# A new order for one block's list of steps in a convolution and SiLU MLP kernel

## The chip, the cores and the metric

The kernel runs on one core of a Trainium2 chip. The metric is the device time of one execution in microseconds; before the change it is 2363.76 us, the median of three runs (2363.1 to 2364.65). TensorE (PE) multiplies matrices, VectorE (DVE) and ScalarE (ACT) work elementwise, GpSimd (POOL) issues the accumulating DMAs of the convolution, and SyncE (SP) issues the other DMAs. Each engine works through its own instructions in order, and engines wait for each other by semaphores.

## The reference

```python
def _attn_ref(x, weight):             # x (8, 4096, 192), weight (8 heads, 7 taps)
    w = softmax(weight, axis=-1)
    x_pad = concatenate([zeros((B, 6, D)), x], axis=1)
    x_unf = x_pad[:, idx, :].reshape(B, S, K, H, group)
    return einsum('hk,bskhg->bshg', w, x_unf).reshape(B, S, D)

def _moe_ref(x, w_in, w_out):         # x (32768, 192), w_in (192, 2048), w_out (2048, 192)
    h = x @ w_in
    g = h * (1.0 / (1.0 + exp(-h)))
    return g @ w_out
```

A causal convolution of seven taps, with one set of weights per head, feeds an MLP with SiLU. All is float32.

## The kernel before

The 32768 tokens are worked in 32 blocks of 1024, each as two strips of 512 (the two halves of the partitions). The up product (192 to 2048) and the down product (2048 to 192) are done with schemes that need fewer multiplications than the plain product and more additions.

The program of a block is a list of short tokens, PLAN. A token names a step and, behind the point, its arguments; a sign in front says which block it belongs to: none is the current block, "-" the one before, "=" two before, "+" the next. The list is run once for each value of b from 3 to 33; START is the same kind of list for what comes ahead. A token whose step is done is skipped. `step` (from L856) calls the functions. Every engine's order is the order in which the list mentions its instructions, so a new list is a new order on every engine and on both DMA queues; within one list there are no other costs or due times.

The tokens:

- P*r*.*g* (`product`, L605 to L640): the up product number r of group g. It uses 64 rows of the array, half A or half B; B has r = 0, 1, 2, 4, 5, 6, 11, 14 (but 14 of group 4 is on A). The two halves work at the same time. Each product is two passes of 512 columns. L.*nk* (`plain`): a plain product, either 512 columns on A, or 256 on each half.
- Three chains of products per group add into one PSUM bank each: 5, 2, 6, 1, 0, 14 (first chain), 3, 9, 7, 4, 8 (second), 12, 10 (third). After most links the bank is read before the next link may add to it: u*o*.*g* (L679) copies the first chain's bank to one of ten buffers on ScalarE, X*o*.*g* and a*o*.*g* (L673) add the second chain's bank to such a copy on VectorE, b*o*.*g* subtracts the third's. S*o*.*g* (L691) and SL are the SiLUs on ScalarE. The groups come in the order 0, 4, 1, 2, 3; banks are shared between them, so P5.2 waits for S3.4, and P5.0 of the next block for S3.3.
- t.*ji* (L714): four sums of SiLU results for each of four j on VectorE, two in one tile. These tiles and the output tile share a ring of three buffers.
- D*i*.*je* (`out_slot`, L746): the down products, 128 rows by 32 columns in four column groups, eight passes each (i = 5 is a quarter as long). D4 and D5 need t of their j, D2 needs t.*j*1, D3 needs t.*j*2 and t.*j*3, D0 and D1 need none.
- z, y, x (ScalarE) and M (VectorE, L824): the accumulators of the down products are merged; o (L834) transposes the result, st (L843) stores it from SyncE.
- ld (L181, SyncE): loads of a later block's tokens; i (L465, VectorE): their transposes; ha (L480 to L487): the six tokens ahead of the block, a POOL copy and a small SyncE DMA.
- v.*ki* (`conv`): tap i of channel third k. For i = 0 ScalarE writes the scaled row (L496); for the others it writes one of the ten buffers that the copies u use too (L499), and a POOL DMA adds that buffer to the row (L500). The buffers go round first in, first out.
- sp (L521, SyncE): the convolved rows are spread to the layout of the products; w (L538, L541, VectorE): differences and sums of these.

In short, a block's up half (P, L, u, X, a, b, S) is followed by its down half (D, t, M), and the taps, loads and spreads of later blocks run beside both.

The lines that turn the list into steps are these; the bars in PLAN split it into slots, which are run one after another.

```python
plan = [slot.split() for slot in PLAN.split("|")]
BACK = {"-": 1, "=": 2, "+": -1}
for t in START.split():
    step(2, t)
for b in range(3, NB + 2):
    for s in plan:
        for t in s:
            step(b, t)
```

Of the kernel before, what the change touches and what calls it, by code (L numbers as in the profile page):

```python
# [17 lines left out]
def kernel(  # L18
# [60 lines left out]


    PLAN = (
        "+ld.1 P5.0 | -P8.3 -S1.4 -a0.2 -S4.3 | -D0.00 -t.01 -S0.2 | -D1.00 -S1.2 =o.2 v.00 "
        "| -D2.01 -t.03 -S5.1 =st.2 | -D2.00 -b5.3 | -D1.20 -sp.0 v.21 -S5.3 | -D4.01 u5.0 "
        "-t.02 -S1.3 | -D5.01 -sp.2 | -D4.00 -t.10 | -D0.20 -t.11 | -D3.01 | -D0.11 -t.12 | "
        "-D1.30 v.22 | -D3.00 +ld.2 -t.13 | -D2.11 -a0.3 | -D5.00 | -D2.10 -t.20 -S0.3 | "
        "-D3.11 v.11 | -D5.10 | -D4.11 -w.0 | -D0.30 v.12 | -D4.10 -t.21 | -D1.11 -t.23 | "
        "-D0.21 | -D0.01 v.23 -w.1 | -D3.10 -t.22 | -D5.21 | -D0.31 | -D5.11 | -D1.10 -t.30 "
        "| -D1.01 -t.31 | -D2.20 | -D2.21 v.13 | -D5.20 | -D4.21 v.01 v.14 | -D4.20 v.24 | "
        "-D1.21 -w.2 | -D3.20 -t.33 | -D2.30 v.02 | -D1.31 -t.32 | -D2.31 -y1.0 | -D5.30 "
        "v.03 | -D0.10 v.25 | -D3.21 -z1.0 v.15 -y0.0 | -D4.31 -y2.0 -w.3 | -D5.31 -M1.0 | "  # L90
        "-D3.30 -x2.1 v.26 -x2.0 | -D4.30 -x2.2 -M2.0 | -D3.31 -w.5 -x0.0 -M3.0 | L.02 | "
        "P2.0 -x2.3 -w.4 | P5.4 | P3.0 u4.0 -M6.0 | L.12 v.16 u5.4 | L.00 | P6.0 -x1.0 -M4.0 "
        "| L.10 u2.0 | P2.4 | L.01 X2.0 | L.11 v.04 u4.4 | P9.0 | P1.0 SL.0 -M5.0 SL.2 | "
        "P6.4 | P13.0 u0.0 X4.0 SL.1 | P5.1 | P3.4 -M7.0 S2.0 +i.2 u2.4 | P0.0 | P7.0 X2.4 | "
        "P11.0 | P12.0 u1.0 a5.0 -o.1 | P9.4 | P1.4 S4.0 b1.0 -st.1 u5.1 | P13.4 | P4.0 X4.4 "
        "u0.4 | P10.0 | P2.1 a1.0 +ld.0 v.05 | P7.4 | P0.4 u4.1 b5.0 | P14.0 | P8.0 u1.4 "
        "v.06 S5.0 | P11.4 | P14.4 a5.4 S3.0 a0.0 S2.4 | P6.1 | P12.4 S3.4 | P4.4 | P3.1 "
        "u2.1 b1.4 S4.4 | P5.2 | P10.4 X2.1 | P1.1 a1.4 u5.2 | P9.1 b5.4 | P2.2 u0.1 | P8.4 "
        "X4.1 | P5.3 u4.2 | P7.1 a0.4 | P0.1 +i.1 u5.3 sp.1 | P12.1 a5.1 | P6.2 u1.1 | P3.2 "
        "-o.0 | P4.1 u2.2 b1.1 | P13.1 | P2.3 a1.1 | P10.1 S2.1 | P1.2 u4.3 X2.2 | P8.1 | "  # L100
        "P11.1 -o.3 u0.2 | P13.2 S1.1 a0.1 | P6.3 S4.1 | P9.2 +i.0 | P0.2 b5.1 u2.3 +ha.0 | "
        "P3.3 S0.0 X4.2 | P1.3 S2.2 | P12.2 u1.2 | P11.2 X2.3 | P7.2 u0.3 b1.2 | P14.1 S4.2 "
        "| P9.3 a5.2 S0.4 | P0.3 -st.0 | P10.2 S1.0 X4.3 | P14.2 u1.3 | P7.3 b5.2 +v.20 "
        "-st.3 | P4.2 S0.1 | P12.3 a5.3 S3.1 | P14.3 +v.10 a1.2 | P13.3 | P4.3 S5.2 b1.3 | "
        "P8.2 S2.3 | P11.3 a1.3 S3.3 | P10.3 S5.4 t.00 S3.2"
    )
    START = (
        "=dp.28 =v.20 =v.10 =dp.44 =v.00 =dp.18 =dp.6 =dp.40 =dp.7 =dp.32 =dp.23 =dp.30 "
        "=dp.13 =dp.2 =dp.20 =dp.24 =dp.15 =dp.35 =dp.14 =dp.33 =dp.11 -ld.1 =dp.37 =dp.36 "
        "=dp.25 -ld.2 =dp.27 =dp.17 -ld.0 =dp.0 =v.11 =dp.34 =v.01 =dp.26 =v.12 =dp.29 =v.21 "  # L110
        "=v.13 =dp.45 =v.22 =dp.21 =v.02 =dp.42 =v.14 =v.03 =dp.39 =v.15 =dp.3 =v.04 =dp.38 "
        "=v.16 =dp.47 =v.23 =sp.1 =v.05 =dp.1 =v.24 =dp.22 -i.1 =dp.12 =v.25 =v.06 =dp.43 "
        "=v.26 =go.2 =sp.0 =dp.19 -i.0 =dp.46 -i.2 =dp.31 -ha.0 =dp.9 =sp.2 =dp.4 =dp.41 "
        "-v.10 -v.00 -v.11 =dp.8 -v.20 -v.01 =dp.5 -v.12 =dp.16 -v.02 =w.0 =dp.10 =w.1 =cp.0 "
        "-L.01 -P5.0 -v.03 =cp.1 -L.02 -P5.4 =w.2 -u5.0 -L.10 =w.3 -u5.4 -P2.0 -P3.0 -v.13 "
        "-P2.4 -u4.0 -v.04 -P6.0 -L.00 -u4.4 -L.12 -u2.0 -L.11 -SL.0 -X2.0 -P6.4 -SL.2 =w.4 "
        "=cp.2 -P9.0 -P1.0 -u2.4 =o.0 -P13.0 -P5.1 -v.14 -u0.0 -X4.0 -P3.4 -P1.4 -S2.0 =w.5 "
        "-SL.1 -P7.0 -P11.0 -u5.1 -X2.4 -u0.4 -P12.0 -P0.0 -a5.0 -v.21 -P13.4 -P0.4 -u1.0 "
        "=o.1 -P4.0 -P9.4 -u1.4 -v.15 -S4.0 -P2.1 -P14.4 -a1.0 -b1.0 -P14.0 -P8.0 -u4.1 -X4.4 "
        "-S3.4 -P6.1 -P10.0 -v.22 -S2.4 -a0.0 -P11.4 -P7.4 -u2.1 -b5.0 -S3.0 -P5.2 -P3.1 "  # L120
        "-S4.4 -a5.4 -P1.1 -P12.4 -u5.2 -X2.1 -P4.4 -u0.1 -P9.1 -b1.4 -P2.2 -a1.4 -P10.4 "
        "-X4.1 -P5.3 -u4.2 -P8.4 =o.2 -P6.2 -b5.4 -P13.1 -u5.3 =st.2 -a0.4 -P0.1 -P7.1 -u2.2 "
        "-v.23 -S2.1 ld.1 -P2.3 -P3.2 -a5.1 -u1.1 -S0.0 -P1.2 -P12.1 -X2.2 -S0.4 -P4.1 -u4.3 "
        "-P13.2 -b1.1 ld.2 -S1.4 -P6.3 -a1.1 -u0.2 -P10.1 -v.24 -P11.1 -u2.3 -P8.1 -b5.1 "
        "-P0.2 -S4.1 -P9.2 -v.05 -S2.2 -a0.1 -P12.2 -P1.3 -u1.2 -X4.2 -S0.1 -P3.3 -P14.1 "
        "-b1.2 -u0.3 -S5.4 -P7.2 -P11.2 -X2.3 -v.16 -P10.2 -P0.3 -S4.2 -a5.2 -sp.1 -P9.3 "
        "-P14.2 -u1.3 -b5.2 -S3.1 -P13.3 -P4.2 -X4.3 -S3.2 -S1.0 i.1 -P14.3 -P12.3 =st.0 "
        "-S1.1 -a1.2 -P11.3 -P7.3 -S5.0 -v.06 -S1.2 -t.00 -D0.00 =st.1 -S3.3 -S2.3 -D1.20 "
        "-b1.3 -S5.1 ld.0 -S4.3 -t.01 -D0.01 -S5.2 -D0.21 -t.02 -D1.11 -sp.0 -a5.3 -D1.10 "
        "-v.25 -t.03 -P8.2 P5.0 +ld.1 -P4.3 -P10.3 -D1.30 -b5.3 -v.26 -D1.00 -a0.2 -sp.2 "  # L130
        "-D4.01 -t.10 -S0.2 -D5.00 -D2.01 i.0 -D4.00 -t.11 -D2.00 i.2 -D5.01 ha.0 -t.13 "
        "-D0.11 -D3.00 -a1.3 +ld.2 -D3.01 -t.12 v.10 -D4.11 -w.0 v.00 +ld.0 -D5.10 v.11 v.20 "
        "-D5.11 -D2.10 u5.0 -t.20 -D0.20 -w.1 -D3.11 -t.21 -D4.10 -w.2 -D2.11 -t.23 -P8.3 "
        "P2.0 -D0.31 -a0.3 -t.22 -D3.10 -S0.3 -S1.3 -D4.21 v.21 -S5.3 u4.0 v.01 -D4.20 -t.30 "
        "-D3.20 -D5.21 -t.31 -D2.20 -D5.20 -D2.21 -D0.10 -t.32 -D2.30 v.02 -D1.01 -t.33 "
        "-D0.30 v.03 -D1.31 v.12 -D2.31 v.04 v.22 -D1.21 v.05 -D3.30 -y1.0 -w.3 -z1.0 -D5.30 "
        "v.13 -D5.31 -D3.31 -x2.0 -M1.0 -x2.1 -D4.31 -x2.2 v.14 -x2.3 -y2.0 -M2.0 -D3.21 "
        "-y0.0 v.06 -D4.30 -x0.0 -w.4 v.23 -x1.0 P3.0 P5.4 -M3.0 L.10 u5.4 -w.5 P6.0 L.02 "
        "-M4.0 L.11 u2.0 L.00 P2.4 X2.0 P1.0 L.01 -M5.0 u4.4 v.15 L.12 u0.0 P6.4 P9.0 SL.2 "
        "SL.0 P0.0 P13.0 X4.0 SL.1 u2.4 -M7.0 P3.4 P5.1 S2.0 +i.0 P7.0 P1.4 u5.1 X2.4 P12.0 "  # L140
        "P11.0 u0.4 a5.0 u1.0 v.24 P9.4 P2.1 S4.0 b1.0 P4.0 P13.4 u4.1 X4.4 P14.0 P10.0 a1.0 "
        "P0.4 P7.4 S3.0 b5.0 v.25 P11.4 P8.0 u1.4 a5.4 S2.4 P6.1 P12.4 a0.0 P14.4 P4.4 u2.1 "
        "b1.4 v.26 P5.3 P3.1 S3.4 a1.4 S4.4 P10.4 P1.1 X2.1 P5.2 P8.4 -M6.0 u0.1 b5.4 P9.1 "
        "P0.1 u5.2 -o.1 u5.3 P13.1 P2.2 X4.1 -st.1 u1.1 +i.2 P12.1 P2.3 u4.2 a0.4 S2.1 P7.1 "
        "P6.2 b1.1 u4.3 P3.2 a5.1 P6.3 u2.2 P10.1 S5.4 X2.2 P4.1 u2.3 S0.4 P9.2 b5.1 P1.2 "
        "S0.0 a1.1 P13.2 P11.1 S1.0 -o.0 u0.2 P8.1 v.16 P1.3 S2.2 S4.1 sp.1 P0.2 P12.2 a0.1 "
        "u0.3 X4.2 S5.0 P3.3 P14.1 u1.2 +i.1 P7.2 P11.2 X2.3 -st.0 b1.2 P9.3 P0.3 S4.2 a5.2 "
        "+ha.0 P10.2 u1.3 X4.3 P4.2 S0.1 P7.3 b5.2 P14.3 S1.1 a1.2 S3.1 P12.3 P14.2 S3.3 a5.3 "
        "P13.3 -o.3 P4.3 S3.2 b1.3 -st.3 +v.10 P8.2 +v.20 a1.3 P10.3 P11.3 S5.2 t.00 S2.3"
    )  # L150
    QUEUE = (0, 4, 1, 2, 3)
    CHAIN_BANKS = ((0, 1, 7, 1, 0), (2, 3, 2, 3, 2), (4, 4, 4, 4, 4))
# [41 lines left out]
    x0 = x.flatten_outer_dims()[TB - pad : TB, :].rearrange("t (k c) -> c k t", k=NK)  # L194
# [651 lines left out]
                )  # L846
            )

    plan = [slot.split() for slot in PLAN.split("|")]
    did, later = set(), []  # L850
    closing = f"S3.{QUEUE[-1]}"
    BACK = {"-": 1, "=": 2, "+": -1}
# [263 lines left out]
```

## Time and profile before

| | |
|---|---|
| time, median of three | 2363.76 us |
| span of the profiled execution | 2358.8 us |
| TensorE busy | 2350.1 us (100%), 17630 matmuls |
| VectorE busy | 1784.5 us (76%) |
| ScalarE busy | 1488.6 us (63%) |
| GpSimd busy | 531.0 us (23%) |
| granted TensorE clock | 0.999 of full speed |
| one regular block: up half, down half | 36.26 us, 36.12 us |

The profiled execution's own time is shown by its span alone, from the first to the last instruction; it is 5.0 us below the median of the runs. In a group of instructions the columns are line, engine, operation, tiles, shape and count, then busy time, mean duration in ns, and the idle time before them with what ended it. A line of waits has the total, the number and the longest. A line of the timeline has start and duration in us, engine, line, operation, tiles and, in brackets, the idle time before it and what ended that. PEld is the load of a matmul's weights.

### The profile page before, as it was taken

How to read it: one execution, taken by the hardware profiler on the slowest of the kernel's cores; microseconds unless marked ns; L12 is line 12 of the kernel's file. 1: busy time of each engine (PE TensorE's matmuls, PEld its weight loads, DVE VectorE, ACT ScalarE, POOL GpSimd, SP SyncE). 2: the span in 40 equal slices, each digit the busy share in tenths (PEclk: the TensorE clock that was granted, in tenths of full speed). 3: DMA queues.
4: the chain of work that ended last, by engine and by line, in shares of the span. 5: the costliest groups of instructions: out<-in, count | busy, mean ns of one | idle time of the engine just before them, and what ended most of it. 6: DMA issues, size and time to landing. Idle time of an engine off the chain costs nothing.

```text
span 2358.8 us, 45531 instructions
## 1 busy us (share of the span) xinstructions
PE 2350.1 (100%) x17630; PEld 1053.1 (45%) x17630; DVE 1784.5 (76%) x2373; ACT 1488.6 (63%) x2779; POOL 531.0 (23%) x672
## 2 busy tenths in 40 slices
PE   9999999999999999999999999999999999999998
PEld 4344444444444444444444454444444444444445
DVE  8898767787777787777877777767778777787676
ACT  5346766667656677566676666765667756667643
POOL 4911122211222112222112221122211222211200
PEclk9999999999999999999999999999999999999999
DMA  7234667656566655666556656556655566565511
GB/s 158 51 66 72 107 106 125 105 103 107 98 121 107 106 105 95 119 116 106 106 106 109 119 99 109 105 99 122 107 106 101 101 116 116 106 109 98 96 23 25
DMA packets 523833, 238.81 MB, mean 101 GB/s; under 512 B 431648, under 2 KB 436768, under 8 KB 523616
## 3 DMA queue, kind: packets, MB, share of 16 engines
q0 software_dynamic: 73024, 133.73, 33.7%
q1 hardware_dynamic: 447392, 101.78, 23.1%
q8 instruction: 138, 2.26, 0.4%
q10 hardware_dynamic: 3200, 0.39, 0.1%
q14 instruction: 79, 0.65, 0.1%
HBM read 31.46 MB, written 25.17 MB: 24 GB/s over the span
## 4 chain that ended last, share of the span: by engine, by line
PE 98%; DVE 1%; DMA 0%; ACT 0%; SPq 0%; issue 0%; ACTq 0%
PE ps L746 47%; PE ps L630 42%; PE ps L647 5%; PE ps L767 2%; PE ps L576 2%; PE ps L1015 1%; DVE t L714 0%; DMA dup<-nat 0%; PE ps L423 0%; ACT g L691 0%; DMA nat<-u 0%; SPq L843 0%; DVE g L673 0%; DVE cmb L163 0%; ACT u L163 0%
## 5 line engine op out<-in xcount | busy, mean ns | idle before, releaser
L500 POOL DMA_DIRECT2D nat<-u x504 | 431.9, 957 | 1598.0 <-ACT u L499 643.4
L630 PE MATMUL ps<-win,wr 64*128 64x512 f32 x1550 | 721.5, 598 | 0.0
L746 PE MATMUL ps<-g,wo 128*32 128x512 f32 x2976 | 703.0, 593 | 0.0
L630 PE MATMUL ps<-win,ws 64*128 64x512 f32 x1550 | 638.3, 599 | 0.9 <-ACT u L679 0.9
L746 PE MATMUL ps<-t,wo 128*32 128x512 f32 (+2 forms) x4528 | 547.8, 446 | 0.0
L679 ACT COPY u<-ps 128x512 f32<-128x512 f32 x775 | 442.5, 587 | 136.7 <-PE ps L630 88.6
L746 PE MATMUL ps<-t,wx 128*32 128x512 f32 x2976 | 495.6, 592 | 0.6 <-DVE t L714 0.5
L630 PE MATMUL ps<-dup,wr 64*128 64x512 f32 x868 | 424.1, 597 | 0.0
L691 ACT ACTIVATE g<-g 128x512 f32<-128x512 f32 x465 | 286.2, 633 | 175.5 <-DVE g L673 175.5
L714 DVE TENSOR_TENSOR t<-g,t 128x1024 f32<-128x1024 f32 x248 | 302.0, 1218 | 109.7 <-PE ps L746 107.4
L714 DVE TENSOR_TENSOR t<-g 128x1024 f32<-128x1024 f32 x248 | 302.5, 1220 | 103.9 <-PE ps L746 82.7
L809 ACT COPY yx<-ps 32x512 f32<-32x512 f32 x150 | 86.8, 579 | 421.5 <-PE ps L746 419.4
L673 DVE TENSOR_TENSOR g<-u,ps 128x512 f32<-128x512 f32 x465 | 314.2, 681 | 42.8 <-PE ps L630 32.0
L499 ACT ACTIVATE u<-xt,taps 128x512 f32<-128x512 f32 x504 | 340.0, 717 | 1.1
L630 PEld LDWEIGHTS ps<-win,wr 64*128 64x128 f32 x1550 | 272.1, 186 | 139.5 <-issue 75.6
L630 PE MATMUL ps<-dup,ws 64*128 64x512 f32 x682 | 328.2, 598 | 0.0
L630 PEld LDWEIGHTS ps<-win,ws 64*128 64x128 f32 x1550 | 255.8, 186 | 135.3 <-issue 58.6
L746 PEld LDWEIGHTS ps<-t,wo 128*32 128x32 f32 x4528 | 188.5, 110 | 273.3 <-issue 266.0
L691 ACT ACTIVATE g<-ps 128x512 f32<-128x512 f32 x465 | 267.8, 599 | 36.2 <-PE ps L630 33.6
L673 DVE TENSOR_TENSOR ps<-u,ps 128x512 f32<-128x512 f32 x310 | 215.0, 694 | 64.3 <-PE ps L630 26.7
L746 PE MATMUL ps<-g,wx 128*32 128x512 f32 x1488 | 250.5, 592 | 0.0
L824 DVE TENSOR_TENSOR cmb<-cmb,ps 96x512 f32<-96x512 f32 x150 | 102.2, 681 | 181.7 <-ACT yx L809 180.7
(92 smaller groups left out, 2010.5 us busy)
## 6 DMA issues: line engine op xcount, KB each, us to landing
nat<-u POOLq DMA_DIRECT2D x504, 256.0 KB, 4.0
dup<-nat SPq DMA_DIRECT2D x345, 128.0 KB, 3.0
nat<-in_x_dram SPq DMA_DIRECT2D x382, 64.0 KB, 2.7
out_dram<-osb SPq DMA_DIRECT2D x376, 64.0 KB, 2.0
raw<-in_moe_w_out_dram SPq DMA_DIRECT2D x8, 384.0 KB, 3.5
raw<-in_moe_w_in_dram SPq DMA_DIRECT2D x12, 192.0 KB, 4.4
ws<-wr POOLq DMA_DIRECT2D x8, 192.0 KB, 5.0
raw<-in_moe_w_in_dram SPq DMA_DIRECT2D x6, 128.0 KB, 3.0
```

Of the source, the lines that this page charges most:

```text
L499: pin(nc.scalar.activation(z, src, AF.Copy, scale=tap))
L500: pin(nc.gpsimd.dma_start(out=dst, in_=z, accum_op=ALU.add))
L576: nc.tensor.matmul(hs[a, n, e], rows(wr[j], e)[:, a, k, :], rows(d, e)[:, n, k, :], start=k == 0, stop=k == NK - 1,)
L630: nc.tensor.matmul(to[:, cols], raw(g, *LEFT[e][r], e), rhs[:, cols], start=first, stop=True, skip_group_check=True,)
L647: nc.tensor.matmul(banks[PLAIN_BANKS[n and 1 + e]][:, cols], rows(wr[j] if own == e else ws[j], e)[:, a, k, :], rows(dups[b], e)[:, SLOT[e ...
L673: pin(nc.vector.tensor_tensor(out_, u, v, op=op))
L679: pin(nc.scalar.copy(us[b, g, o][:, cols], t1[:, cols]))
L691: pin(nc.scalar.activation(h, src, AF.Silu))
L714: pin(nc.vector.tensor_tensor(t[i // 2][:, i % 2, :], u, v, op=ALU.subtract))
L746: nc.tensor.matmul(accs[b][at][SQ * q : SQ * q + SQ, to], lhs[:, e, SQ * k : SQ * k + SQ], rhs[:, e, ts(q, TB // 4) if i == 5 else to], st ...
L809: pin(nc.scalar.copy(to, acc[3 * (name[0] == "x") + k][n:P, :]))
L824: pin(nc.vector.tensor_tensor(out_, u, v, op=ALU.add))
```

## The change

PLAN, the list of a block, is replaced by another order of the same 300 tokens, without bars, and START gets five more tokens at its end (the new list has them in another iteration). The list is now split at blanks. START is otherwise the same text in lines of other lengths, cut here to its end. No step is added, removed or altered.

```diff
--- before.py
+++ after.py
@@ -79,74 +79,69 @@


     PLAN = (
-        "+ld.1 P5.0 | -P8.3 -S1.4 -a0.2 -S4.3 | -D0.00 -t.01 -S0.2 | -D1.00 -S1.2 =o.2 v.00 "
-        "| -D2.01 -t.03 -S5.1 =st.2 | -D2.00 -b5.3 | -D1.20 -sp.0 v.21 -S5.3 | -D4.01 u5.0 "
-        "-t.02 -S1.3 | -D5.01 -sp.2 | -D4.00 -t.10 | -D0.20 -t.11 | -D3.01 | -D0.11 -t.12 | "
-        "-D1.30 v.22 | -D3.00 +ld.2 -t.13 | -D2.11 -a0.3 | -D5.00 | -D2.10 -t.20 -S0.3 | "
-        "-D3.11 v.11 | -D5.10 | -D4.11 -w.0 | -D0.30 v.12 | -D4.10 -t.21 | -D1.11 -t.23 | "
-        "-D0.21 | -D0.01 v.23 -w.1 | -D3.10 -t.22 | -D5.21 | -D0.31 | -D5.11 | -D1.10 -t.30 "
-        "| -D1.01 -t.31 | -D2.20 | -D2.21 v.13 | -D5.20 | -D4.21 v.01 v.14 | -D4.20 v.24 | "
-        "-D1.21 -w.2 | -D3.20 -t.33 | -D2.30 v.02 | -D1.31 -t.32 | -D2.31 -y1.0 | -D5.30 "
-        "v.03 | -D0.10 v.25 | -D3.21 -z1.0 v.15 -y0.0 | -D4.31 -y2.0 -w.3 | -D5.31 -M1.0 | "
-        "-D3.30 -x2.1 v.26 -x2.0 | -D4.30 -x2.2 -M2.0 | -D3.31 -w.5 -x0.0 -M3.0 | L.02 | "
-        "P2.0 -x2.3 -w.4 | P5.4 | P3.0 u4.0 -M6.0 | L.12 v.16 u5.4 | L.00 | P6.0 -x1.0 -M4.0 "
-        "| L.10 u2.0 | P2.4 | L.01 X2.0 | L.11 v.04 u4.4 | P9.0 | P1.0 SL.0 -M5.0 SL.2 | "
-        "P6.4 | P13.0 u0.0 X4.0 SL.1 | P5.1 | P3.4 -M7.0 S2.0 +i.2 u2.4 | P0.0 | P7.0 X2.4 | "
-        "P11.0 | P12.0 u1.0 a5.0 -o.1 | P9.4 | P1.4 S4.0 b1.0 -st.1 u5.1 | P13.4 | P4.0 X4.4 "
-        "u0.4 | P10.0 | P2.1 a1.0 +ld.0 v.05 | P7.4 | P0.4 u4.1 b5.0 | P14.0 | P8.0 u1.4 "
-        "v.06 S5.0 | P11.4 | P14.4 a5.4 S3.0 a0.0 S2.4 | P6.1 | P12.4 S3.4 | P4.4 | P3.1 "
-        "u2.1 b1.4 S4.4 | P5.2 | P10.4 X2.1 | P1.1 a1.4 u5.2 | P9.1 b5.4 | P2.2 u0.1 | P8.4 "
-        "X4.1 | P5.3 u4.2 | P7.1 a0.4 | P0.1 +i.1 u5.3 sp.1 | P12.1 a5.1 | P6.2 u1.1 | P3.2 "
-        "-o.0 | P4.1 u2.2 b1.1 | P13.1 | P2.3 a1.1 | P10.1 S2.1 | P1.2 u4.3 X2.2 | P8.1 | "
-        "P11.1 -o.3 u0.2 | P13.2 S1.1 a0.1 | P6.3 S4.1 | P9.2 +i.0 | P0.2 b5.1 u2.3 +ha.0 | "
-        "P3.3 S0.0 X4.2 | P1.3 S2.2 | P12.2 u1.2 | P11.2 X2.3 | P7.2 u0.3 b1.2 | P14.1 S4.2 "
-        "| P9.3 a5.2 S0.4 | P0.3 -st.0 | P10.2 S1.0 X4.3 | P14.2 u1.3 | P7.3 b5.2 +v.20 "
-        "-st.3 | P4.2 S0.1 | P12.3 a5.3 S3.1 | P14.3 +v.10 a1.2 | P13.3 | P4.3 S5.2 b1.3 | "
-        "P8.2 S2.3 | P11.3 a1.3 S3.3 | P10.3 S5.4 t.00 S3.2"
+        "v.01 -S4.3 -P13.3 -P10.3 -sp.2 v.11 P5.0 -a1.3 -P8.3 v.02 -t.00 -t.01 -a0.2 -D1.31 "
+        "-D0.01 =st.1 -S5.1 -D1.11 -S5.4 -D1.00 -D1.20 -S2.3 -D2.01 -D0.21 -t.02 -t.03 -D2.00 "
+        "-S0.2 -D3.01 -b5.3 -t.10 v.22 -t.11 -D2.10 -D5.00 -D0.11 -D1.10 -D4.01 -a0.3 -D3.00 "
+        "-S0.3 v.12 -D4.00 v.13 v.23 -D0.30 v.24 -t.13 -D0.20 -D0.00 -S1.3 -S1.2 v.03 v.04 "
+        "-D5.01 -D4.10 -D4.11 -t.12 -D3.11 -S5.3 -D2.11 -t.20 -t.21 -D0.31 -sp.0 -w.0 -D5.10 "
+        "-D0.10 -y0.0 -D3.10 -D2.21 -D5.11 -D2.20 -t.23 -D4.21 -D1.21 v.14 v.15 -D1.01 -w.1 "
+        "-D4.20 -t.22 -D3.21 -w.2 -t.30 -D1.30 u5.0 -z1.0 -D5.20 -w.3 -w.5 v.05 -t.31 -t.33 "
+        "-D5.31 v.25 v.06 -w.4 -D5.30 -D5.21 -x2.1 +ld.2 -D2.31 +ld.0 +i.0 +ld.1 -y1.0 -D2.30 "
+        "-t.32 -x2.2 -D3.31 -M1.0 -M2.0 -y2.0 -M6.0 v.26 -x2.0 v.16 -D3.30 -D3.20 -D4.30 -D4.31 "
+        "-x1.0 P2.0 L.02 -x2.3 u4.0 P5.4 -M3.0 -M4.0 -x0.0 +i.2 P3.0 L.01 P6.0 u5.4 u2.0 -o.1 "
+        "X2.0 L.00 SL.0 -M5.0 L.12 P2.4 u4.4 L.11 L.10 SL.1 +i.1 -M7.0 SL.2 P1.0 u0.0 P9.0 P6.4 "
+        "u2.4 P13.0 X4.0 S2.0 P5.1 u5.1 P3.4 -o.2 P7.0 P0.0 u1.0 X2.4 P11.0 S4.0 P12.0 a5.0 "
+        "P9.4 P1.4 u0.4 P4.0 P13.4 P2.1 b1.0 P10.0 X4.4 P7.4 a1.0 P0.4 -st.2 -o.3 u4.1 S2.4 "
+        "u1.4 P8.0 b5.0 S5.0 P11.4 P6.1 a5.4 a0.0 P12.4 b1.4 u2.1 P14.4 P14.0 S3.4 P3.1 S3.0 "
+        "P4.4 P5.2 S4.4 X2.1 P10.4 u5.2 P1.1 u0.1 a1.4 P9.1 S1.4 b5.4 -st.3 P8.4 P2.2 u4.2 P0.1 "
+        "X4.1 P7.1 a0.4 S0.4 a5.1 S0.0 u1.1 P12.1 b1.1 P5.3 u5.3 P6.2 u2.2 +ha.0 P13.1 S2.1 "
+        "P4.1 P3.2 S1.0 a1.1 X2.2 P2.3 u4.3 P11.1 +v.00 sp.1 P10.1 P8.1 a0.1 P1.2 -o.0 -st.0 "
+        "b5.1 S4.1 P6.3 P9.2 X4.2 u0.2 P13.2 u2.3 P0.2 S2.2 P3.3 P1.3 P12.2 P7.2 P11.2 X2.3 "
+        "u1.2 P14.2 b1.2 P9.3 u0.3 P0.3 P10.2 +v.20 a5.2 P4.2 S4.2 X4.3 P7.3 S0.1 P14.1 u1.3 "
+        "P14.3 +v.10 b5.2 P12.3 S3.3 S3.2 a1.2 P8.2 +v.21 a5.3 P4.3 S1.1 S3.1 b1.3 P11.3 S5.2"
     )
     START = (
...
-        "P13.3 -o.3 P4.3 S3.2 b1.3 -st.3 +v.10 P8.2 +v.20 a1.3 P10.3 P11.3 S5.2 t.00 S2.3"
...
+        "b5.2 P14.3 S1.1 a1.2 S3.1 P12.3 P14.2 S3.3 a5.3 P13.3 -o.3 P4.3 S3.2 b1.3 -st.3 +v.10 "
+        "P8.2 +v.20 a1.3 P10.3 P11.3 S5.2 t.00 S2.3 -o.2 -st.2 S1.4 +v.00 +v.21"
     )
     QUEUE = (0, 4, 1, 2, 3)
     CHAIN_BANKS = ((0, 1, 7, 1, 0), (2, 3, 2, 3, 2), (4, 4, 4, 4, 4))
@@ -846,7 +841,7 @@
                 )
             )

-    plan = [slot.split() for slot in PLAN.split("|")]
+    plan = [PLAN.split()]
     did, later = set(), []
     closing = f"S3.{QUEUE[-1]}"
     BACK = {"-": 1, "=": 2, "+": -1}
```

## The prediction

> **What bounds the kernel now.** I read the page first, then busy time by stretch, groups by shape, waits, and the timeline of single products.
>
> ```profile
> PE 2350.1 (100%) x17630; PEld 1053.1 (45%) x17630; DVE 1784.5 (76%) x2373; ACT 1488.6 (63%) x2779; POOL 531.0 (23%) x672
> ...
> PE 98%; DVE 1%; DMA 0%; ACT 0%; SPq 0%; issue 0%; ACTq 0%
> ...
> nat<-u POOLq DMA_DIRECT2D x504, 256.0 KB, 4.0
> ...
> out_dram<-osb SPq DMA_DIRECT2D x376, 64.0 KB, 2.0
> ```
>
> TensorE is the chain. But "busy" counts a moment in which one half of the array works and the other waits, so 100% hides what a new order can win. The stretches of one regular block (14), up half and down half, and the end of the one and start of the next:
>
> ```profile
> 1046.56:1082.82 36.26, 36.26 (x172) 20.13 (x168) 30.17 (x47) 30.91 (x59) 4.37 (x6) 1.00 0.52 90
> 1082.82:1118.94 36.12, 36.12 (x385) 12.04 (x384) 23.89 (x26) 16.95 (x31) 11.19 (x13) 1.00 0.68 119
> ```
>
> The first column is the length. A block is 72.38 us at full clock (1.00). In the up half VectorE (30.17) and ScalarE (30.91) are close behind TensorE.
>
> ```profile
> L630 PE MATMUL ps<-win,wr 64*128 64x512 f32 x1550 | 721.5, 598 | 0.0
> L679 ACT COPY u<-ps 128x512 f32<-128x512 f32 x775 | 442.5, 587 | 136.7 <-PE ps L630 88.6 <-DMA nat<-u 28.3 <-ACT yx L804 6.2
> L673 DVE TENSOR_TENSOR g<-u,ps 128x512 f32<-128x512 f32 x465 | 314.2, 681 | 42.8 <-PE ps L630 32.0
> L499 ACT ACTIVATE u<-xt,taps 128x512 f32<-128x512 f32 x504 | 340.0, 717 | 1.1
> ```
>
> ```profile
> PEld ps L630 <- DVE ps L673: 48.6, 180, 0.8
> PEld ps L630 <- ACT u L679: 29.0, 88, 1.3
> PEld ps L630 <- ACT g L691: 27.7, 59, 0.6
> PEld ps L630 <- DVE g L673: 15.3, 48, 0.8
> ACT u L679 <- DMA nat<-u: 28.3, 24, 2.4
> ```
>
> These are the weight loads that waited for a bank to be read. The last line is a copy (u4.2 in nearly every block) that waits until the tap v.06 has left its buffer. Single products, three of block 14 and two of block 2:
>
> ```profile
> 1062.88 0.29 PEld L630 LDWEIGHTS ps<-dup,wr 64*128 64x128 f32 x2 [0.58 <-ACT g L691]
> ...
> 1066.06 0.18 PEld L630 LDWEIGHTS ps<-win,wr 64*128 64x128 f32 x1 [0.24 <-DVE ps L673]
> ...
> 1066.58 1.07 ACT L679 COPY u<-ps 128x512 f32<-128x512 f32 x2 [1.10 <-DMA nat<-u]
> ```
>
> ```profile
> 210.14 0.18 PEld L630 LDWEIGHTS ps<-dup,ws 64*128 64x128 f32 x1 [0.30 <-DVE u L673]
> 210.15 0.29 PEld L630 LDWEIGHTS ps<-dup,wr 64*128 64x128 f32 x2
> 210.15 0.69 PE L630 MATMUL ps<-dup,wr 64*128 64x512 f32 x1
> ...
> 210.51 0.59 PE L630 MATMUL ps<-dup,ws 64*128 64x512 f32 x1
> ...
> 210.68 0.59 PE L630 MATMUL ps<-dup,wr 64*128 64x512 f32 x1
> ...
> 211.11 0.59 PE L630 MATMUL ps<-dup,wr 64*128 64x512 f32 x1
> ```
>
> Block 2 shows the rules of the queue. P10.3 (dup,ws, half A) waits at 210.14; P11.3 (dup,wr, half B), listed behind it, may not load before that, but then starts at once, 0.36 us before P10.3, whose half is still busy. So a wait holds everything listed behind it, and a half with a product in hand does not. Starts in one half are 0.43 us apart (210.68, 211.11); a product is two passes, 0.858 us.
>
> **The price of a wait.** The up half has 40.5 products for each half of the array: 40.5 x 0.858 = 34.75 us. Of the 36.26 us, 0.30 is the turn from and to the down products (0.11, 0.08, and 0.107 for a weight load in the open: the first two passes of the block start 0.54 apart, not 0.43). The remaining 1.2 us are waits on half A, the later one. By the starts in block 14 they are P9.0 0.07, P14.4 0.02, P10.4 0.15, P9.1 0.02, P7.1 0.16, P7.3 0.16, and each pays the open weight load of 0.107 again: 0.58 + 6 x 0.107 = 1.22.
>
> **The change part by part.** No instruction is added or taken away; all counts stay. I walk the new list from the end of the down half (time 0) with gaps of this trace: 0.20 to 0.27 from a product's end to the reader's start, 0.05 from the reader's end to the next weight load, and 0.61 (VectorE) or 0.48 (ScalarE) from start to start of neighbours. A product counts as done only when all listed before it are.
>
> P9.0: in the new list P6.0 stands directly behind P3.0 and L.01, and ScalarE has only x2.3, u4.0, x0.0 and u5.4 before u2.0 (v.16 and x1.0 leave the place). u2.0 runs 3.13 to 3.71, X2.0 3.74 to 4.44; half A is free at 4.93. The wait goes (0.17). What is late instead is P6.0: u4.0 ends at 1.91, 0.03 after half B is free, 0.14 with the load, on the half that has slack.
>
> P14.4 now stands behind P12.4: due at 14.39, u1.4 ends 13.68. The wait goes (0.13).
>
> P10.4 still stands behind P5.2, which waits for S3.4. S3.4 no longer queues behind v.06 and S2.4: 15.45 to 16.06, load 16.12, half A free 16.11. 0.12 left of 0.26.
>
> P9.1 waits for X2.1 (16.38 to 17.08; half A free 17.08): 0.155, was 0.13. P7.1 waits for X4.1 (18.37 to 19.06; free 18.96) and P7.3 for X4.3 (29.81 to 30.50; free 30.40): 0.26 each, as before, since each is its half's own chain of product, addition, product.
>
> Sum 0.79 against 1.22: **0.41 us less per block**, with the down half at 35.83 instead of 36.26. Both ends for this: no gain if every saved wait is handed to the next link, 1.2 us if all six go. The walk lies in between and I take it.
>
> The down half must stay without a wait. D1.31 to D1.20 need no sum t, so VectorE may be late. Its first tight one is D2.10, due at 35.85 + 0.11 + 9 x 0.858 = 43.7. t.10 takes the buffer of the output tile, so st.1 must have landed. On SyncE st.1 now stands behind sp.2, whose third DMA waits for P10.3 (34.9); issues are about 0.53 apart, so st.1's last goes at 37.4 and lands 2.0 (median) to 3.0 (a spread's median) later, at 40.4. VectorE reaches t.10 at 34.4 + 4 x 1.14 + 2 x 0.61 = 40.2, t.11 ends at 42.7: 1.0 us to spare, cost nothing; without this cover each us is a us of the block. t.33 may start when D4.20 is done and has 1.93 us until D5.31, needing 1.47; t.32 with w.4 and the moved i.0 ahead has 4.29 and needs 3.83. Nothing again, with 0.4 to spare.
>
> The taps: all 18 (17 of them from the head of the list on; 717 ns on ScalarE and one POOL DMA each) end with v.16 before the next up half, instead of v.04 to v.06 lying in it. POOL takes them in order, and a tap waits for the landing of the one before on its row, 3.8 to 4.7 us apart in block 14. v.06 issues at about 70, lands by 75, 3 us into the next block; its buffer now goes to u5.1 at 8.0, not to u4.2. That cover of 5 us removes the long up halves: blocks 8, 9, 11, 12, 18, 21 and 30 were over the regular one by 0.17, 0.89, 0.36, 0.27, 0.47, 0.98 and 0.28, **3.4 us together**. The price is a fuller DMA in the down half (0.68 now, 0.52 in the up half).
>
> Loads and i: ld.2, ld.0, ld.1 follow sp.0 on SyncE, about 41 to 47 with 2.7 to land; i.0, VectorE's first user, comes near 65. ha.0's POOL copy finds POOL idle, its DMA moves behind st.3 (about 14), 9 us before v.00. o.1 to o.3 move earlier, into places where VectorE waits for ScalarE; X4.0 then ends at 6.90, P7.0 is due at 7.51. M4 and M3 run at the seam, needed at 3.7. All nothing.
>
> Last block: its held products make D2.10 come three products earlier, 41.1 against t.11 at 42.7: 1.6 us lost once.
>
> Sum: 29 blocks (3 to 31) x 0.41 = 11.9, plus 3.4, less 1.6: 13.7. The profiled execution has a span of 2358.8, 5.0 below the median of 2363.76 (what lies around it); the change is in the span, so 2363.8 - 13.7 = **2350**.
>
> **Rivals.** (1) Handed on: the chains of product, copy, product (P5.2, u5.2, P2.2, u4.2) are the same in both lists and half B gains only 0.05 there; were half A drawn back to it at each meeting, the steady gain would be under 0.15 us: 2360 to 2364. For: P9.1, P7.1, P7.3 remain. Against: half B has 0.4 us in hand at the end.
>
> (2) Slower: st.1 too late. In block 14 one spread DMA in the run of seven took 1.75 us on SyncE to issue. Should that fall ahead of st.1, or landing take 5 us, t.11 ends past 43.7. It decides against the change from a lateness of 1.0 + 0.4 us; at 1.2 us of stall the block is 0.8 us longer: 2363.8 + 23 - 2 = 2385. For: t.10 waits for stores today (10.4 us in 22 waits of t for osb). Against: the slack.
>
> (3) Larger gain: P7.1 and P7.3 miss by 0.15 each; a little less latency drops them and their loads: 0.9 us per block, 2363.8 - 26 - 2 = 2336.
>
> (4) Slower still: halves that start strictly in list order. The old list alternates A and B; the new one has P2.3 P11.1 (B, B) before P10.1 P8.1 (A, A), P1.2 P6.3 before P9.2 P13.2, and L.00, L.12 before P2.4. Each order flip would cost a half up to 0.86: by my walk 2.0 us per block, 1.6 over before, 2408. The pair of block 2 speaks against it: P11.3 started 0.36 before P10.3. What I can't see is a half with two products in hand; if only one fits, P10.1 loads when P2.3 starts, in time, because half A lags.
> [...]
>
> **How the numbers follow.** A measurement of this kernel tells about 0.2% (4.7 us) from no change. Forecast, 2343 to 2357: 0.50; larger gain 0.13; handed on, within 0.2%: 0.15, with another 0.03 of it still faster; slower by (2) 0.09, by (4) 0.04, by fuller DMA delaying the taps past 5 us 0.06. Faster 0.66, same 0.15, slower 0.19. The range 2337 to 2369 leaves out half of the larger gain's lower end (0.06) and most of the slower cases (0.14).
>
> **What would show it.** After: up half near 35.85, down half 36.1; waits of L630 on DVE ps down by about a third, those on ACT u nearly gone; the copies' wait for nat<-u from 28 to under 5; t's waits for osb unchanged; no wait of L746 on t. Wrong if an up half has a new wait at P6.0, P10.1 or P12.3, or D2.10 waits for t.11.

## The result, and the profile after

The changed kernel takes 2512.72 us (median of 4 runs, 2507.01 to 2521.62) against 2363.86 us before: ratio 1.0633, 95% interval 1.0611 to 1.0656. The forecast was 2350. The profiled execution took 2507.0 us, with a span of 2505.3 and a granted clock of 0.981. Line numbers of the changed kernel are those of the old one less 5.

The page of the changed kernel: busy time by engine, the chain that ended last, and two kinds of DMA (count, size, median us from issue to landing).

```profile
PE 2382.8 (95%) x17630; PEld 1134.4 (45%) x17630; DVE 1798.6 (72%) x2373; ACT 1501.0 (60%) x2779; POOL 534.0 (21%) x672
...
PE 85%; DMA 5%; SPq 4%; DVE 4%; issue 2%; ACT 0%; DVEq 0%; POOL 0%; ACTq 0%; POOLq 0%
...
nat<-u POOLq DMA_DIRECT2D x504, 256.0 KB, 4.4
...
out_dram<-osb SPq DMA_DIRECT2D x376, 64.0 KB, 2.0
```

TensorE is no longer busy throughout, and DMA and SyncE stand on the chain. The median landing of a store is still 2.0: it hides the few that matter. Busy time by stretch splits block 14 into up half and down half (length, then busy time and count of PE, PEld, DVE, ACT, POOL, then clock, DMA share, GB/s):

```profile
1109.45:1145.21 35.76, 35.76 (x173) 23.14 (x169) 28.00 (x43) 29.16 (x55) 3.45 (x4) 1.00 0.34 60
1145.21:1188.62 43.41, 38.47 (x386) 11.88 (x385) 26.52 (x29) 19.17 (x35) 13.13 (x16) 0.92 0.77 132
```

These stretches begin with the first product of each half. Counted so, block 14 of the kernel before is

```profile
1046.67:1082.83 36.16, 36.16 (x173) 20.13 (x169) 30.07 (x47) 30.92 (x59) 4.37 (x6) 1.00 0.52 90
1082.83:1119.05 36.22, 36.22 (x386) 12.04 (x385) 23.99 (x26) 16.94 (x31) 11.19 (x13) 1.00 0.68 120
```

(in the prediction the up half begins 0.11 earlier, with the turn from the down half). The up half did what was forecast: 0.40 us less, where 0.41 was forecast. The down half, 36.22 before, takes 43.41. The waits (us in all, times, longest):

```profile
PEld ps L741 <- DVE t L709: 162.0, 86, 6.2
...
PE ps L741 <- DVE t L709: 114.1, 28, 5.3
...
DVE t L709 <- DMA out_dram<-osb: 78.4, 16, 6.2
...
DVE t L709 <- DMA dup<-nat: 54.4, 11, 5.8
...
PEld ps L625 <- ACT u L674: 38.8, 117, 0.6
...
PEld ps L625 <- DVE ps L668: 18.0, 75, 0.7
```

A down product waits for t 28 times, 4 us on average, once in each block from 3 to 31 but one (block 30, where POOL issues no tap in the down half and SyncE issues the stores every 0.6 us), and t waits for a DMA: the stores from the output tile (for 11 of the waits the profile names the spreads, which stand next to the stores on the same queue). Single steps of block 14, SyncE first (start, time for all issues of the row), then VectorE and TensorE around the stall:

```profile
1143.94 1.75 SPq L516 DMA_DIRECT2D dup<-nat  x3
1145.73 4.13 SPq L838 DMA_DIRECT2D out_dram<-osb  x3
1149.97 3.31 SPq L516 DMA_DIRECT2D dup<-nat  x3
```

```profile
1149.00 0.68 DVE L668 TENSOR_TENSOR g<-g,ps 128x512 f32<-128x512 f32 x1
1155.54 1.23 DVE L709 TENSOR_TENSOR t<-g 128x1024 f32<-128x1024 f32 x1 [5.86 <-issue]
1156.80 1.22 DVE L709 TENSOR_TENSOR t<-g,t 128x1024 f32<-128x1024 f32 x1
```

```profile
1151.67 0.60 PE L741 MATMUL ps<-t,wx 128*32 128x512 f32 x3
...
1152.10 1.04 PE L741 MATMUL ps<-t,wo 128*32 128x512 f32 x8
1158.08 1.08 PE L741 MATMUL ps<-t,wx 128*32 128x512 f32 x3 [4.94 <-DVE t L709]
1158.10 1.06 PE L741 MATMUL ps<-g,wo 128*32 128x512 f32 x1
```

The three stores of st.1 take 4.13 us to issue, against 1.41 for the three of st.2 in the down half of the old kernel, where they go out ahead of the spreads. Their landing in block 14 is this, in the line of the store's DMAs (changed kernel first, old kernel below; the trace has it for two of the three, so the middle number is their mean):

```profile
DMA to landing us min/median/max: 5.4/6.1/6.9
```

```profile
DMA to landing us min/median/max: 1.8/1.9/2.0
```

So t.10 runs at 1155.54, VectorE having been idle since 1149.68; t.11 follows, and D2.10 starts 5.1 us late. The passes behind it last 1.08 us, where those of the same shape took 0.60 ahead of the stall. Three stretches of the changed kernel around this (columns as above):

```profile
1143.40:1149.40 6.00, 6.00 (x49) 2.01 (x49) 5.97 (x7) 6.00 (x12) 2.54 (x3) 1.00 0.71 126
1149.40:1155.40 6.00, 3.74 (x36) 0.91 (x28) 0.28 (x1) 1.02 (x2) 1.73 (x2) 1.00 1.03 190
1155.40:1158.10 2.70, 0.03 (x4) 0.03 (x4) 2.53 (x3) 0.00 (x0) 0.00 (x0) 0.51 1.14 183
```

The DMA engines are full (1.03, 1.14), and the granted clock is 0.51 in the last stretch, ahead of which TensorE had been idle since 1153.14. From the starts of the products in blocks 3 to 31: the waits of D2.10 sum to 119.2 us (28 waits, 1.7 to 5.5), the slow products behind them lose 40.4 us more.

### The profile page after: what moved, and what is told of

Its sections match the earlier page's. It is cut to its first block, busy times and chain, and to the rows that moved or that the text cites. A ratio compares the mean times of both kernels' runs of the same rounds, so it can differ in the third digit from the quotient of the medians.

```text
span 2505.3 us, 45594 instructions
## 1 busy us (share of the span) xinstructions
PE 2382.8 (95%) x17630; PEld 1134.4 (45%) x17630; DVE 1798.6 (72%) x2373; ACT 1501.0 (60%) x2779; POOL 534.0 (21%) x672
## 4 chain that ended last, share of the span: by engine, by line
PE 85%; DMA 5%; SPq 4%; DVE 4%; issue 2%; ACT 0%; DVEq 0%; POOL 0%; ACTq 0%; POOLq 0%
PE ps L625 40%; PE ps L741 38%; DVE t L709 3%; SPq L838 3%; PE ps L642 3%; DMA out_dram<-osb 3%; PE ps L762 2%; PE ps L571 2%; DMA dup<-nat 2%; SPq L516 1%; PE ps L1010 0%; DVE g L668 0%; DMA nat<-u 0%; PE ps L418 0%; DVE u L668 0%
## 5 line engine op out<-in xcount | busy, mean ns | idle before, releaser
L741 PE MATMUL ps<-g,wo 128*32 128x512 f32 x2976 | 733.9, 626 | 0.0
L625 PE MATMUL ps<-win,wr 64*128 64x512 f32 x1550 | 706.5, 597 | 0.2 <-DVE g L668 0.2
L625 PE MATMUL ps<-win,ws 64*128 64x512 f32 x1550 | 627.9, 595 | 0.0
L674 ACT COPY u<-ps 128x512 f32<-128x512 f32 x775 | 448.1, 587 | 136.0 <-PE ps L625 124.4
L709 DVE TENSOR_TENSOR t<-g 128x1024 f32<-128x1024 f32 x248 | 301.6, 1217 | 166.0 <-DMA out_dram<-osb 78.4
L625 PE MATMUL ps<-dup,wr 64*128 64x512 f32 x868 | 414.3, 590 | 0.0
L625 PE MATMUL ps<-dup,ws 64*128 64x512 f32 x682 | 313.4, 594 | 0.6 <-DVE u L668 0.6
L625 PEld LDWEIGHTS ps<-win,ws 64*128 64x128 f32 x1550 | 248.6, 186 | 124.0 <-ACT u L674 38.3
L741 PEld LDWEIGHTS ps<-t,wx 128*32 128x32 f32 x2976 | 118.6, 111 | 371.2 <-issue 213.3
L668 DVE TENSOR_TENSOR ps<-u,ps 128x512 f32<-128x512 f32 x310 | 215.1, 694 | 92.0 <-PE ps L625 38.8
```

Of the source, the lines that this page charges most:

```text
L625: nc.tensor.matmul(to[:, cols], raw(g, *LEFT[e][r], e), rhs[:, cols], start=first, stop=True, skip_group_check=True,)
L668: pin(nc.vector.tensor_tensor(out_, u, v, op=op))
L674: pin(nc.scalar.copy(us[b, g, o][:, cols], t1[:, cols]))
L709: pin(nc.vector.tensor_tensor(t[i // 2][:, i % 2, :], u, v, op=ALU.subtract))
L741: nc.tensor.matmul(accs[b][at][SQ * q : SQ * q + SQ, to], lhs[:, e, SQ * k : SQ * k + SQ], rhs[:, e, ts(q, TB // 4) if i == 5 else to], st ...
```

## Experiments

Ratios are against the kernel before, run again beside each group of experiments (its medians: 2365.17, 2365.53 and 2365.06 us).

**st.1 in the up half before.** One token is moved; in block 14 its three stores go out 9 to 11 us earlier on SyncE (not 20, as the expectation has it):

```diff
-... -a0.2 -D1.31 -D0.01 =st.1 -S5.1 -D1.11 ...
+... -a0.2 -D1.31 -D0.01 -S5.1 -D1.11 ...
-... P1.2 -o.0 -st.0 b5.1 S4.1 ...
+... P1.2 -o.0 -st.0 -st.1 b5.1 S4.1 ...
```

> New list with st.1 alone moved: from behind the spreads sp.2 in the down half to right behind st.0 in the up half before, so its three stores go out about 20 us earlier, ahead of sp.2. Theory (the whole loss is st.1 queued behind sp.2 in a full DMA, so that t.10 and with it D2.10 come late): in the changed kernel D2.10's waits sum to 119 us and the slow products right behind them to 40 us; both go, 2512.7 - 159.6 = 2353, and by my forecast of the up half 2350; range 2347 to 2357. Down half back to 36.2 from 42.3, up half stays 35.76, no wait of the down products for t, granted clock 0.99 or more. Rival (the fuller DMA and the earlier taps delay something else as well, a load, a spread or a tap, which the wait at D2.10 only hides): the wait goes but a new one takes its place, 2380 to 2450. Second rival (t.10 is late for another reason than the stores): 2490 or more.

Measured: 2347.83 us (5 runs, 2347.28 to 2348.49) against 2365.17 for the kernel before, ratio 0.993, interval 0.9918 to 0.9943; span 2345.6, clock 0.999. The theory holds: the whole loss goes with the place of st.1, and this version is 0.7% faster than the kernel before. Block 14 by stretch, and the waits of the copies and of the down products that are left:

```profile
1041.46:1077.21 35.75, 35.75 (x172) 23.07 (x169) 28.01 (x43) 29.14 (x55) 3.61 (x6) 1.00 0.47 80
1077.21:1113.43 36.22, 36.22 (x386) 12.04 (x385) 26.44 (x29) 19.17 (x35) 11.12 (x15) 1.00 0.77 132
```

```profile
ACT u L674 <- DMA nat<-u: 10.4, 15, 1.4
PE ps L741 <- DVE t L709: 1.6, 1, 1.6
```

The DMA share of the down half, 0.77, is that of the changed kernel, and the spreads are as slow as there (up to 1.55 us to issue, up to 7.4 to land). In a stretch of 6 us with a DMA share of 1.00 TensorE is nevertheless busy throughout:

```profile
1081.00:1087.00 6.00, 6.00 (x68) 2.01 (x64) 3.64 (x5) 3.71 (x7) 1.91 (x3) 1.00 1.00 184
```

So the full DMA cost nothing here, where no store was in it that t.10 needs.

**st.1 right ahead of the spreads.** The smallest move that puts the stores ahead of the spreads, eleven tokens earlier (the expectation says 13):

```diff
-... -P10.3 -sp.2 v.11 P5.0 ... -D0.01 =st.1 -S5.1 ...
+... -P10.3 =st.1 -sp.2 v.11 P5.0 ... -D0.01 -S5.1 ...
```

> New list with st.1 moved by 13 tokens only: from behind D0.01 to right ahead of sp.2, where SyncE has nothing to wait for. It is the smallest edit that puts the stores ahead of the spreads; taps, spreads and products stay. Theory (the place behind sp.2 is the whole cause): as with st.1 in the up half, 2346 to 2352, no wait of the down products for t but the last block's 1.7. Rival (the stores must be out of the stretch with full DMA altogether, or the spreads, now a little later, delay a tap): 0.3 us or more per block, 2356 or more.

Measured: 2348.17 us, ratio 0.9926 (0.9911 to 0.9941). As forecast by the theory, but this is the experiment above a second time. No other token between st.0 and sp.2 gives SyncE anything to do, and it waits for nothing there, so the stores go out straight behind st.0 (six in one row), the last of them 6 us ahead of the first tap, and land after 2.0 us (median of 25 blocks). The run above has the same order, shown below it:

```profile
1067.31 3.05 SPq L838 DMA_DIRECT2D out_dram<-osb  x6
1070.45 11.26 SPq L516 DMA_DIRECT2D dup<-nat  x7
```

```profile
1067.23 3.05 SPq L838 DMA_DIRECT2D out_dram<-osb  x6
1070.38 11.51 SPq L516 DMA_DIRECT2D dup<-nat  x7
```

Both moves take the stores from behind the spreads and out of the stretch with the taps at once. The rival named here, that the stores must be out of that stretch altogether, is thus not tested in the new list.

**The taps later, st.1 where it is.**

```diff
-v.01 -S4.3 -P13.3 -P10.3 -sp.2 v.11 P5.0 -a1.3 -P8.3 v.02 -t.00 ... -t.10 v.22 -t.11 ...
+-S4.3 -P13.3 -P10.3 -sp.2 P5.0 -a1.3 -P8.3 -t.00 ... -t.10 -t.11 ...
-... -D3.00 -S0.3 v.12 ... P8.2 +v.21 a5.3 ...
+... -D3.00 -S0.3 v.21 v.01 v.11 v.02 v.22 v.12 ... P8.2 a5.3 ...
```

> New list with st.1 where it is, behind sp.2, but the five taps v.21, v.01, v.11, v.02, v.22 (ScalarE and a 256 KB POOL DMA each) moved from before and among the first down products to behind S0.3, behind t.11 and D2.10. Theory A (the stores are late because taps, spreads and stores want the DMA engines at the same time, share 1.03 and 1.14): spreads then issue in 0.5 each, st.1's stores too, they land after 2 to 3 us, D2.10's wait is under 1 us instead of 4.4, granted clock back to 0.99, and the time is 2360 to 2385; the taps end about 10 us later, which may bring back a wait of a copy for a tap's buffer in the up half (up to 1 us per block). Theory B (the place behind the spreads alone makes the stores late, whatever the taps do): D2.10 still waits 3 to 4.4 us, 2450 to 2510.

Measured: 2496.8 us (1.0557, interval 1.054 to 1.0573). The time is theory B's, the mechanism is A's: the stores behind the same spreads land after 2.1 us (median of 25 blocks), the waits of D2.10 sum to 2.8 us, and every down half but a few is 36.22. The loss has moved to the up half, which takes 39.8 to 43.5 us in place of 35.76:

```profile
ACT u L674 <- DMA nat<-u: 191.2, 173, 3.2
```

The line was 2.7 us in the changed kernel and 10.4 with st.1 early. The copies u wait for buffers that late taps still hold, about six times per block. I had priced the move at up to 1 us per block; the 5 us that v.06 had in hand don't hide taps that start 8 to 10 us later (the first five of block 14).

**A square of two edits in the old list.** The edits are its st.2 behind sp.2; its taps v.21, v.00, v.11, v.01, v.22 ahead; and both.

```diff
-... -D2.01 -t.03 -S5.1 =st.2 | -D2.00 ... -D5.01 -sp.2 | -D4.00 ...
+... -D2.01 -t.03 -S5.1 | -D2.00 ... -D5.01 -sp.2 =st.2 | -D4.00 ...
```

```diff
-+ld.1 P5.0 | -P8.3 -S1.4 ... =o.2 v.00 | ... -sp.0 v.21 -S5.3 | ...
++ld.1 P5.0 | v.21 v.00 v.11 v.01 -P8.3 -S1.4 ... =o.2 | ... -sp.0 v.22 -S5.3 | ...
```

> Old list with one token moved: st.2 from ahead of the spreads sp.2 to right behind them, so that its three stores stand on SyncE where st.1 stands in the new list. Nothing of the new order is in it. Theory (a store queued behind sp.2 lands 5 to 7 us after its issue and holds t.10): in the old kernel the seven spreads take 5.56 us to issue, the stores now go at about 8 to 9 us into the down half, land at 11 to 15, t.11 ends at 13 to 17 where D2.11 is due at 10.5; 2.6 to 6.7 us per block of 28, and up to 1.7 more where slow products follow: 2437 to 2600, D2.11 waits for t. Rival (the stores land late only because the new list's taps come earlier; the old list's taps come behind): the stores land within 3 us, the wait is under 1 us and the time 2364 to 2385.

> Old list with taps moved ahead: v.21, v.00, v.11, v.01 to right behind P5.0, at the head of the list, and v.22 from behind D1.30 to behind sp.0; st.2 stays ahead of sp.2. With the kernel before, the old list with st.2 late, and the next run (both edits) it makes a square of two edits. The taps put 2.9 us of ScalarE (4 x 0.717) ahead of the SiLUs that the first down products need, so this alone may cost 0 to 2.5 us per block: 2364 to 2437. Theory (stores are late only where they stand behind the spreads and the taps run at the same time): the stores of st.2 land after about 2 to 3 us here and no down product waits for t behind them.

> Old list with both edits: the taps ahead as in the run beside it, and st.2 right behind sp.2. Theory (both together make the loss, in any list): where each edit alone leaves the stores landing after some 2 to 3 us, they now land 4 us or more after their issue, the spreads take over 0.6 us each to issue, t.10 and t.11 come late and D2.11 waits 2 to 5 us: 28 x 2 to 28 x 5 = 56 to 140 us over the run beside it, and up to 1.7 us more per block where slow products follow. Rival (something else in the new list makes its stores late): within 10 us of the run beside it.

The three stores of st.2 in blocks 5 to 29 (the median over the blocks of each block's median landing, as far as landings are recorded, and issue), with the times:

| old list | time, us | ratio (95%) | landing, us | issue of one, us |
|---|---|---|---|---|
| as it is | 2363.9 | 1 | 2.0 | 0.49 |
| stores behind the spreads | 2362.2 | 0.9985 (0.9975 to 0.9994) | 2.1 | 0.53 |
| taps ahead | 2432.6 | 1.0298 (1.0276 to 1.0319) | 3.4 | 0.71 |
| both | 2444.2 | 1.0336 (1.032 to 1.0351) | 5.4 | 1.34 |
| new list, for comparison | 2512.7 | 1.0633 (1.0611 to 1.0656) | 6.3 | 1.30 |

For the landing this says what it was meant to: behind the spreads alone a store is as quick as before, beside the taps it takes 3.4 us, and with both 5.4. For the time it does not. In all three edited lists (block 14) the semaphores of the stores are waited for ahead of t.12 in place of t.10 (the ring of three buffers is handed out otherwise), and t.12 is wanted later; so the old list with its stores behind the spreads lost nothing, where I expected 73 us at least, and both edits cost 12 us more than the taps alone, between the two expectations. The 67 us of the taps alone are ScalarE's: the four taps stand ahead of the SiLU that t.01 needs, and D2.01 waits 2.15 to 2.42 us in each block; behind 5 of these waits slow products lose 1.7 us more. How much a late store costs is thus shown in the new list only.

**D2.10 nine products later**, stores, spreads and taps untouched:

```diff
-... -t.11 -D2.10 -D5.00 ... -D0.20 -D0.00 -S1.3 ...
+... -t.11 -D5.00 ... -D0.20 -D0.00 -D2.10 -S1.3 ...
```

> New list with D2.10 alone moved nine products later, behind D0.00; stores, spreads and taps as in the changed kernel, so t.10 and t.11 are as late as there (t.11 ends at about 12 us into the down half). Theory (TensorE loses only what D2.10 waits, and VectorE has the time to catch up in the rest of the down half): D2.10 is now due 14.4 us into the down half, after t.11; the waits go to under 0.5 us per block, the slow products behind them go too, 2350 to 2368. Stores still land 5 to 7 us after their issue. Rival (the lateness is passed on by VectorE to t.13, t.12, t.20 and so to D3.11, D2.11 or D2.21): 1 to 3 us per block stay, 2380 to 2440.

Measured: 2403.98 us (1.0174, interval 1.0153 to 1.0195), the rival's range. The stores land after 6.3 us (median) as before, D2.10 waits once (0.8 us), but VectorE hands its lateness on by a way that neither side had named: a0.3 stands behind t.11 on VectorE, S0.3 on ScalarE waits for a0.3, and D0.30 waits for S0.3. In block 14 (waits in 1110 to 1125 us):

```profile
ACT g L686 <- DVE g L668: 8.3, 1, 8.3
...
PE ps L741 <- ACT g L686: 1.7, 1, 1.7
```

D0.30 loses 30.5 us in 27 blocks. S0.3 also holds the taps behind it on ScalarE, and the up halves of this run are up to 6 us longer (in 16 of 27 blocks): the copies' wait for tap buffers is 60.9 us in all. So work queued behind the late t counts too, not D2.10 alone.

**D2.10 three products later.**

```diff
-... -t.11 -D2.10 -D5.00 -D0.11 -D1.10 -D4.01 ...
+... -t.11 -D5.00 -D0.11 -D1.10 -D2.10 -D4.01 ...
```

> New list with D2.10 alone moved three products later, behind D1.10, that is 1.93 us (0.215 + 2 x 0.858). It tells a wait's own length from the slow products that follow it. In the changed kernel the waits of D2.10 sum to 119 us and the slow products behind them to 40 us; the waits of 3.3 to 3.95 us mostly lost nothing behind them. Theory A (TensorE runs at half clock only after it has been idle for about 4 us): waits fall to about 2.45 each, none reaches 4 us, and all 40 us of slow products go as well: 2512.7 - 27 x 1.93 - 40 = 2421, range 2412 to 2430, granted clock 0.99 or more. Theory B (slow products follow any long wait, or come from the full DMA at that moment): only the 1.93 us per block go, 2512.7 - 52 = 2461, range 2450 to 2470, granted clock still about 0.98.

Measured: 2429.29 us (2425.81 to 2430.53; 1.0272, interval 1.0258 to 1.0286). The sum lies in theory A's range, but the single waits refute it. They are 1.6 to 3.0 us, 64.6 us in 27 blocks, none reaches 4 us, and still 10 of the 27 have slow products behind them, 16.4 us in all. Two stretches right behind such a wait, block 7 (2.30 us of waiting) and block 8 (2.73):

```profile
598.40:601.80 3.40, 3.40 (x20) 0.81 (x24) 0.49 (x1) 2.87 (x5) 0.86 (x1) 0.52 0.82 132
```

```profile
674.75:678.20 3.45, 3.45 (x36) 1.06 (x40) 0.51 (x1) 2.91 (x5) 0.85 (x1) 1.00 1.03 152
```

The shorter wait was followed by half clock (0.52), the longer one by full clock (1.00), with the DMA fuller in the second (1.03 against 0.82). So neither the length alone nor the full DMA decides (theory B falls too, as 17 waits lost nothing). Where a wait loses something, it is 1.70 to 1.72 us in most blocks of both kernels, by my estimate 3.4 us at half clock (twice the loss; block 7's stretch above is 3.40 us at 0.52); in the others it is 1.5 to 2.5.

## Why the prediction was wrong, point by point

**The step that failed** is the down half's first tight one: "st.1's last goes at 37.4 and lands 2.0 (median) to 3.0 (a spread's median) later, at 40.4 ... 1.0 us to spare, cost nothing". In block 14 the last issue starts at 39.05 (counted as in the prediction), as each takes 1.28 to 1.48 us and not 0.53, and it lands 6.9 us later, at 45.9; t.11 ends at 48.7 against 42.7. VectorE was free for t.10 when the walk said (40.3, forecast 40.2). The durations had been medians of the old kernel, whose stores go out ahead of its first tap, with one tap beside its seven spreads. The new list puts more 256 KB taps there:

```profile
1144.21 0.84 POOL L495 DMA_DIRECT2D nat<-u  x1 [30.51 <-ACT u L494]
1146.35 0.86 POOL L495 DMA_DIRECT2D nat<-u  x1 [1.29 <-ACT u L494]
1147.45 0.84 POOL L495 DMA_DIRECT2D nat<-u  x1 [0.24 <-ACT u L494]
1152.56 0.86 POOL L495 DMA_DIRECT2D nat<-u  x1 [4.26 <-DMA nat<-u]
```

In the prediction's count POOL issues v.21, v.01 and v.11 at 34.9, 37.0 and 38.1 and v.02 at 43.2. I walked the taps to their end, at v.06, and SyncE by itself, and never laid the two queues over each other. That the taps are needed for it is shown by moving them away (2.1 us, no wait), that the place of st.1 is needed by moving it (2.0 us, no wait). How late the stores would be in the new list ahead of the spreads but beside the taps is not shown; in the old list they landed after 3.4 us there.

**The right rival had the wrong price.** "Slower: st.1 too late" named the place and the two conditions, a slow issue and a landing of 5 us; both came, in every block with taps. Its price was 1.2 us of stall, 0.8 per block; the stall is 4.35 us on average (117.5 us in 27 blocks, without block 31's) and 1.5 more is lost to slow products. Together these 157.9 us account for the difference between the profiled executions of the changed kernel and of the version with st.1 early, 2507.0 - 2347.3 = 159.7. Its chance, 0.09, was far too low: one slow spread in seven in the old trace, 1.75 us beside a tap, was the sign of it, and I took it for an accident. "Fuller DMA" I had only as a delay of the taps.

**The up half was right.** Forecast 0.41 us per block (the prediction's "down half at 35.83 instead of 36.26" means the up half): with st.1 early, a regular block takes 71.98 us, against 72.37, so 0.39. The long up halves (3.4 us) are gone: from block 4 on all are 35.75 to 35.79. Last block: D2.10 waits 1.75 us, forecast 1.6. Sum 29 x 0.39 + 3.4 - 1.75 = 13.0; the span fell from 2358.8 to 2345.6, by 13.2. That these lie so close is partly luck: blocks 3 and 31 gained 0.8 us less than the others, and a down half that was 1.0 us too long (block 18), which the forecast had not counted, became regular too. The forecast, 2350, is what the new list gives once its st.1 is not late.

**Its signs.** The copies' wait for tap buffers fell from 28.3 to 2.7 us (forecast under 5; 10.4 with st.1 early), the weight loads' wait for DVE ps from 48.6 to 18.0 us, more than the third forecast. Wrong: the wait for ACT u did not vanish, it rose from 29.0 to 38.8 us, without making the up half longer than forecast. Wrong too: "t's waits for osb unchanged" (10.4 to 78.4). D2.10 waiting for t.11 was named as what would refute the forecast, and did.

**The other rivals.** Halves that start strictly in list order (2408) is refuted: with that many flips of order the up half is 35.76. The walk counts a product as done only when all listed before it are; of this one pair of the old kernel speaks, that of block 2: P11.3's last pass begins at 210.68 and P10.3's at 210.94, and by the semaphore updates in the trace they are done at 211.59 and 211.54. The handed-on gain is refuted too. The larger gain did not come: P7.1 and P7.3 still wait 0.16 us each with the load of 0.10 behind it, in the version with st.1 early.

## What to carry to other kernels

When a reordering moves transfers, lay all queues over one another on one time axis: a duration from a stretch where the DMA share was 0.55 (1084.80 to 1088.20 of the old block 14, landing 1.9 us) was no price for one where it was 1.03 (landing 6.1), and the page's median landing, 2.0 in both kernels, hid the three stores that matter. A store that frees a buffer belongs ahead of bulk transfers, as soon as its data are there (2347.83 us against 2512.72), and work that feeds the array should not be queued on its engine behind the instruction that waits for that buffer (D0.30 lost 30.5 us behind a0.3 and S0.3). A slack of 1.0 us was none against a landing of 6.9 us where 2.0 to 3.0 had been counted.

## What the runs showed of the hardware

In the old list the landing of a 64 KB store, 2.0 us, rose with its place and its company, and more than additively: 2.1 us behind seven spreads, 3.4 beside taps, 5.4 with both; the issue itself on SyncE goes from 0.5 to 1.3 us.

TensorE's granted clock fell to about half around some of the waits: to 0.51 in block 14 of the changed kernel (5.1 us of waiting), to 0.52 in block 7 with D2.10 three products later (2.30 us). In the changed kernel waits up to 3.95 us could still lose nothing, and every longer one lost; with D2.10 three products later 10 of the 27 waits, all between 1.6 and 3.0 us, lost. The usual loss was 1.70 to 1.72 us. What decides whether a wait loses something was not shown.
